# Softmax attention beside linear attention on one core: the DMA-made exponent copy against a third copy on VectorE

## The chip, the core and the metric

The kernel runs on one core of a Trainium2 chip. TensorE (PE) multiplies matrices into PSUM, ScalarE (ACT) and VectorE (DVE) do element-wise work and read PSUM, GpSimd (POOL) does element-wise work in SBUF, and SyncE (SP) issues most transfers; GpSimd can issue transfers too. PSUM has eight banks of 128 x 512 fp32. Each engine runs its own instruction list in order, and semaphores tie the lists together. The metric is the device time of one execution in microseconds, lower being better.

## The reference

Two attention layers on different inputs, with 2048 rows, width 512 and 32 heads of 16; their outputs stand side by side.

```
A:  q,k,v = split(x @ wqkv);  p = softmax(q k^T / 4);  out_A = (p v) @ wo
B:  q,k,v = split(x @ wqkv);  pq = q w_phi;  pk = k w_phi            (per head)
    phi(t) = [softmax(t), softmax(-t)]                               (32 features)
    kv = phi(pk)^T v;  z = sum_s phi(pk);  out_B = (phi(pq) kv / (phi(pq) z + 1e-6)) @ wo
```

A has 32 x 2048 x 2048 = 134 million exponentials and is by far the larger part. B is linear in the sequence.

## The kernel before

**Units and key tiles.** Part A is cut into 32 units: 4 query chunks of 512 rows times 8 groups of 4 heads. A unit has 16 key tiles of 128 keys, so there are 512 key tiles. For each, PE makes four score pieces (one head each, 128 keys x 512 queries, `kq`, L771), an engine takes their exponentials, and PE multiplies these with the values (`pv_task`, L778); a 17th column of ones in the value tile `VP` makes the softmax's row sums. Four heads sit side by side in the array, in row strips for the scores and in column strips for the products.

**Two ways to the exponential.** ACT takes it with its own function, two or three pieces an instruction (`act_exp`, L1003), into the tile `pT`. DVE [...]writes a scaled and rounded score as a 16-bit integer into `rg` (L1061) and the bits are then read as fp16: that is a power of two with a straight line between powers. To mend the straight line, the kernel takes four such numbers, whose integers are shifted by 0, 256, 512 and 768 (`sh`), each multiplied with a value tile scaled by a fitting weight (`VP` and the three `VJ`), and lets PE add up the four products. So a key tile on DVE (`dve_kt`) needs four conversions, three shifted copies, and four products on PE instead of one. Only the key tiles in `DK`, five of each unit, may go this way; 136 of the 512 did.

**How the copies are made.** Copies 2 and 3 are one DVE instruction each on the whole tile of 128 x 2048 integers (L1079). Copy 1 is made by the DMA engines: SP fills a slot of `rg` with the constant 256 from `sh_d` in DRAM (`pf`, L1071), and GpSimd then issues a transfer from the first tile to that slot which adds as it writes (`ac`, L1073). `rg` has eight slots: `NB = 3` for first tiles, `NJ = 2` for DVE's copies, `ND = 3` for the DMA's. A first tile's slot becomes free when its product and all of its copies are done.

**End of a unit.** DVE copies the products' bank to `X` (L831). SP moves the row sums to `sums` (L839), DVE takes reciprocals (`rin`, L847), SP writes these to DRAM (`scr`, L850) and reads them back broadcast over the partitions (`Yd`, L853), and GpSimd multiplies (L869), into `OT` for even groups or `Oo` for odd ones, whose rows SP then moves into `OT` (L876). `X` and `Yd` have two slots each. When a chunk's eight groups are done, PE applies `wo` (L1124), DVE evacuates to `OA` (L1139) and SP stores.

**Part B** runs in the gaps of part A: projections with folded weights, exponentials on ACT (L1226, L1293), sums, divisions and products on DVE and GpSimd (L1231 to L1340), its output projection on PE (L1352).

**What sets the order.** A small planner in the program (`_Sched`) fixes every engine's instruction list ahead of time. Each kind of work is a stream of tasks with an assumed duration. The planner always places the task that can start first, shifted by a weight of its stream; the weights come from `_W`, and `_AT` changes them after so many key tiles of progress. The planner also decides which key tiles DVE gets (`src_d`, `cut`, `lead`, `dg`), and it adds products with a tile of zeros where PE would be idle too much (`filler`, L805). DVE's copies and GpSimd's instructions are kept apart in the plan (`port`). It assumes 0.59 us for a DVE copy, and 5.0 us for a DMA copy after 1.1 us on GpSimd.

Of the kernel before, what the change touches and what calls it, by code (L numbers as in the profile page):

```python
# [161 lines left out]
class _Sched:  # L162
# [147 lines left out]
    def _place(self, t, start):  # L310
# [41 lines left out]
        if t.then is not None:  # L352
# [4 lines left out]
          b=-0.067, op=-0.004, dx=-0.205, dxe=-0.193, dev=-0.248, dop=-0.359, dn=-0.214, da=-0.165, dad=0.113,  # L357
# [2 lines left out]
          aqf=-0.089, aot=-0.317, age=0.03, early=0.0, guard=0.346, cut=5, lead=6, b0=0.286, b1=0.54, b2=0.99,  # L360
          p0=8, p1=30, p2=6.012, el=2, va=8, ka=4, dm=0.4, force=0.41, fill=0.575, dg=9.0)
_AT = (
    (24, dict(qa=-0.125, qd_o=0.203, da=-0.187, df=-0.11, aot=-0.35)),
    (48, dict(qd_o=0.356, pa_n=2, dev=-0.104, kv=0.078)),
    (72, dict(tp=-0.294, qd_r=0.065, qd_o=0.321, pa_w=0.123, dx=-0.302, dred=-0.087, dv=-0.001, dmn=0.142,
         akf=0.041, aot=-0.47, lead=7)),
    (96, dict(qa=-0.159, da=-0.247, kf=-0.02, y=-0.153, t=0.012, df=0.019, dred=-0.109, dd=-0.017, dob=0.004,
         aqf=0.01, guard=0.283, force=0.419, dg=3.0)),
    (120, dict(tp=-0.226, qa=-0.04, qd_r=0.073, qd_o=0.235, pa_n=3, pa_w=0.053, dx=-0.205, dev=-0.248, da=-0.165,
         kf=-0.03, kv=0.004, y=-0.203, t=0.061, df=-0.163, dred=-0.076, dv=-0.053, dd=0.003, dob=-0.078, dmn=0.041,  # L370
         akf=-0.019, aqf=-0.089, aot=-0.317, guard=0.346, lead=6, force=0.41, dg=9.0)),
    (144, dict(dy=0.009, aot=-0.297, guard=0.274, lead=5)),
    (168, dict(qd_r=-0.022, pa_n=2, dn=-0.167, dv=-0.125, dd=-0.063, akf=-0.032, aqf=-0.171, fill=0.586, dg=3.0)),
    (192, dict(qd_r=0.097, y=-0.085)),
    (216, dict(qa=-0.039, qd_r=0.115, pj=-0.014, pa_n=3, dxe=-0.133, dev=-0.306, dn=-0.214, dad=0.045, y=-0.203,
         dv=-0.014, dy=-0.02, dd=0.003, dmn=-0.032, akf=-0.019, aqf=-0.089, aot=-0.317, guard=0.346, el=3,
         fill=0.597, dg=1.5)),
    (240, dict(qd_r=0.14, pa_n=4, pd_w=0.153, da=-0.114, df=-0.266, dob=-0.175, dmn=0.08, aqf=-0.079, guard=0.248)),
    (264, dict(dx=-0.377, dad=0.025, akf=-0.119)),
    (288, dict(tp=-0.301, pa_n=5, pd_w=0.016, dad=-0.034, kf=0.01, v=0.055, qf=-0.094, y=0.004, df=-0.336,  # L380
         dmn=0.121)),
    (312, dict(op=0.063, dad=-0.024)),
    (336, dict(y=-0.045, df=-0.392)),
    (360, dict(op=-0.021, kf=0.025, o=0.205, dd=0.064)),
    (384, dict(kf=-0.024, guard=0.269)),
    (408, dict(dxe=-0.193, t=0.163, cut=4, lead=4)),
    (432, dict(qd_o=0.185, pj=0.163, b=-0.08, op=-0.003, dop=-0.46, v=0.03, kv=-0.04, y=0.001, t=0.272, o=0.12,
         df=-0.395, dd=-0.028, aot=-0.427, lead=5, dg=0.8)),
    (456, dict(tp=-0.219, qd_r=0.146, pa_n=6, b=-0.094, op=-0.009, dn=-0.244, kv=-0.137, t=0.295, dob=-0.155,
         dmn=0.138, aqf=-0.026, guard=0.311, cut=5, lead=4, force=0.427)),  # L390
    (480, dict(tp=-0.226, qd_r=0.115, qd_o=0.235, pj=-0.051, pa_n=4, pd_w=0.104, b=-0.067, op=-0.004, dx=-0.255,
         dev=-0.139, dop=-0.359, dn=-0.214, da=-0.165, dad=0.113, kf=-0.03, v=0.039, kv=0.004, qf=-0.012, y=-0.203,
         t=0.061, o=0.243, df=-0.163, dv=-0.053, dd=0.003, dob=-0.125, dmn=0.041, akf=-0.019, aqf=-0.089,
         aot=-0.383, guard=0.483, lead=6, el=2, force=0.415, fill=0.575, dg=9.0)),
    (504, dict(qd_o=0.219, pa_n=2, dx=-0.277, dev=-0.248, df=-0.133, dob=-0.029, aot=-0.317, guard=0.346,
         force=0.41, fill=0.62)),
)
# [8 lines left out]
def _main_path(nc, es, P, dsem, flag, A_x, A_wqkv, A_wo, B_x, B_wqkv, B_w_phi, B_wo, out):  # L406
# [1 line left out]
    S, H, NG, NKT, NQC = 2048, 32, 8, 16, 4  # L408
    NU = NG * NQC
    VW = H * 17  # L410
    NPT = 13
    NB, NJ, ND = 3, 2, 3
    NR = NB + NJ + ND
    DK = (3, 6, 9, 12, 15)
    units = [(g, c) for c in range(NQC) for g in range(NG)]
    MM = _Sched.MM
# [3 lines left out]
    def sb(name, shape, dt):  # L420
        return es.enter_context(nc.sbuf_tensor(name, shape, dt))
# [44 lines left out]
    QT = sb("QT", [128, NQC, 4, 512], BF)  # L466
    KT = sb("KT", [128, NG, S], BF)
    OT = sb("OT", [128, 2, 4, 512], BF)
    Oo = sb("Oo", [128, 1, 512], BF)
    VP = sb("VP", [128, NKT, VW], BF)  # L470
    VJ = sb("VJ", [128, _NPH - 1, len(DK), VW], BF)
    WOp = sb("WOp", [128, 4, 512], BF)
# [4 lines left out]
    Yd = sb("Yd", [128, 2, 512], F32)  # L477
    sums = sb("sums", [128, 512], F32)
    rin = sb("rin", [128, 2, 16], F32)
    OA = sb("OA", [128, 1, 512], BF)  # L480
    zer = sb("zer", [128, 32], BF)
    scr = nc.dram_tensor("scr", [NU, 4, 512], F32)
    sh_d = nc.dram_tensor("sh_d", [1, 2048], U16)

    A_bank = [_Slot(0), _Slot(3)]
    G = [_Slot(5), _Slot(6), _Slot(7), _Slot(2)]
    beside = {0: (G[3], 0), 3: (G[3], 2)}
    pt_sl = [_Slot(i) for i in range(NPT)]
    rg_sl = [_Slot(i) for i in range(NR)]
    ri_sl, rj_sl, rd_sl = rg_sl[:NB], rg_sl[NB:NB + NJ], rg_sl[NB + NJ:]  # L490
    x_sl = [_Slot(i) for i in range(2)]
    y_sl = [_Slot(i) for i in range(2)]
    oo_sl = [_Slot(i) for i in range(1)]
    r_sl = [_Slot(i) for i in range(2)]
    oa_sl = [_Slot(i) for i in range(1)]

    def left_in(slots, lo, wt):
        def f(_):
# [29 lines left out]
    po_n = SC.stream("pool", 0.0)  # L528
    po_k = SC.stream("pool", 0.0)
    po_v = SC.stream("pool", 0.02)  # L530
    po_a = SC.stream("pool", -0.3)
    sp_q = SC.stream("sp", 0.0)
    sp_pf = SC.stream("sp", -0.05)
    ac_q = SC.stream("act", -1.0)
    sp_b = SC.stream("sp", 0.01)
    sp_bo = SC.stream("sp", 0.01)
# [15 lines left out]
    def dma(key, fn, n=1):  # L552
        def emit(t, toks):
            tok = None
            for i in range(n):
                tok = P.dma("sp", key(t) if callable(key) else key, lambda e, i=i: fn(e, t, i), toks)
            return tok
        return emit

    def sw(key, fn):  # L560

        def emit(t, toks):
            return P.dma("pool", key(t), lambda e: fn(e, t), toks)
        return emit

    d_pf = [dsem("pf%d" % i) for i in range(ND)]
    d_ac = [dsem("ac%d" % i) for i in range(ND)]

    def put(s, t):
        s["q"].append(t)  # L570
        return t
# [33 lines left out]
    for s in y_sl:  # L605
        s.toks = [t_yd1]
    t_zer = P.op("pool", lambda e: e.memset(zer[:], 0.0))
    t_sh = P.op("pool", lambda e: e.memset(rg[0:1, NR - 1, :], float(sh[1])))
    l_sh = load("shc", lambda e, i: e.dma_start(sh_d[:], rg[0:1, NR - 1, :]), 0.5, pre=[t_sh])
    rd_sl[-1].toks = [t_sh]  # L610
    t_vp1 = P.op("pool", lambda e: e.memset(VP[:].rearrange("p k (h j) -> p k h j", j=17)[:, :, :, 16], 1.0))
    SC.free["pool"] = 5.0
    SC.free["pe"] = 1.0
# [151 lines left out]
    def v0(h):  # L765
        return 17 * h - 16 * (h % 2)
# [263 lines left out]
    def dve_kt(u, kt):  # L1030
# [40 lines left out]
        pf = put(sp_pf, _Task("sp", 0.5, dma(lambda t: d_pf[t.res["j"].idx - NB - NJ], lambda e, t, i: e.dma_start(  # L1071
            rg[:, t.res["j"].idx, :], sh_d[:].broadcast_to([128, 2048]))), [l_sh], lat=3.3, need=[("j", rd_sl, 1, 1)]))
        ac = put(po_a, _Task("pool", 1.1, sw(lambda t: d_ac[pf.res["j"].idx - NB - NJ], lambda e, t: e.dma_start(  # L1073
            rg[:, pf.res["j"].idx, :], rg[:, q0.res["i"].idx, :], accum_op=ALU.add)), [pf] + firsts, lat=5.0,
            rel=[lambda: [q0.res["i"]]]))
        put(pe_pd, pv_task(u, [ac, vj_ready[(kt, 1)]], lambda h: VJ[:, 0, k, v0(h):v0(h) + 32],
                           lambda r: tile(pf.res["j"], r), [lambda: [pf.res["j"]]]))
        for j in range(2, _NPH):
            ad = put(dv_ad, _Task("dve", 0.59, one("dve", lambda e, t, j=j: e.tensor_scalar(  # L1079
                rg[:, t.res["j"].idx, :], rg[:, q0.res["i"].idx, :], float(sh[j]), 32767.0, ALU.add, ALU.min)),  # L1080
                firsts, lat=DL, need=[("j", rj_sl, 1, 1)], rel=[lambda: [q0.res["i"]]], port=True))
# [65 lines left out]
    woB = sb("woB", [128, 4, 512], BF)  # L1147
    Wf = sb("Wf", [128, 2, 4, 512], BF)
    e_k = sb("e_k", [128, 2, 1024], BF)
    eT = sb("eT", [128, 2, 2, 512], BF)  # L1150
    KVacc = sb("KVacc", [128, 272], F32)
    KVbd = sb("KVbd", [128, 8, 144], BF)
    rmin = sb("rmin", [128, 64], F32)
# [8 lines left out]
    o_b = [wfl[:, 4352 + 512 * k:4864 + 512 * k] for k in range(2)]  # L1162
    oT_b = [e_k[:, k, 0:512].rearrange("p (t s) -> p t s", s=128) for k in range(2)]
    ob_b = [e_k[:, k, 512:1024] for k in range(2)]
    eT_b = [eT[:, k] for k in range(2)] + [Wf[:, 1, 2 * k:2 * k + 2, :] for k in range(2)]
    et_sl = [_Slot(k) for k in range(4)]
    d_ob = [dsem("ob0"), dsem("ob1")]

    pe_kf, pe_v, pe_kv, pe_qf, pe_y, pe_t, pe_o = (SC.stream("pe", x) for x in "kf v kv qf y t o".split())
# [1217 lines left out]
```

## Time and profile before

| What | Value |
|---|---|
| Three runs | 944.51, 947.09, 932.78 us; median 944.51 |
| Profiled execution | 944.51 us, of which the span of instructions is 942.8 us |
| Busy | PE 788.4, ACT 749.9, DVE 690.0, POOL 312.7 us |
| Mean clock granted to TensorE | 0.869 of full |
| Bytes moved by DMA | 166.05 MB, mean 176 GB/s |
| Of these read from or written to HBM | 83.12 and 4.45 MB |
| Prefill of copy 1, SP | 136 times, 5.6 us to landing |
| Accumulation of copy 1, GpSimd | 136 times, 6.0 us to landing |
| DVE conversions, copies | 544 of 681 ns, 272 of 736 ns (means) |

A row of the groups names line, engine, operation, output and inputs, shape and count; after the bar stand the busy time in us, the mean of one in ns, and the engine's idle time just before these instructions with what ended it. A row of the waits names who waited for what, the total in us, how often, and the longest. PE is shown as matmuls (PE) and weight loads (PEld). Records of two instructions that follow each other can overlap a little, so the busy time of a group can be less than count times mean.

### The profile page before, as it was taken

Reading aid. Unit: us, or ns where it says so; the run is one execution under the profiler, and the core shown is the slowest. Engines: PE = TensorE matmul, PEld = TensorE weight load, DVE = VectorE, ACT = ScalarE, POOL = GpSimd, SP = SyncE. Lnnn points to the kernel's source line nnn. Section 1 sums busy time; section 2 is a strip of 40 time slices with the busy share of each in tenths; the row PEclk is TensorE's granted clock in tenths of the full one; section 3 lists DMA queues with packets and bytes.
Section 4 is the critical chain, followed back from the end, with each engine's and each line's share of the span. In section 5 each row is a group of like instructions: output and inputs, shape, how many; then the busy total and the mean of one; then the engine's idle time right before and its main releaser. Section 6 shows DMA issues by size and latency. Waiting matters only on the chain.

```text
span 942.8 us, 17573 instructions
## 1 busy us (share of the span) xinstructions
PE 788.4 (84%) x7172; PEld 220.1 (23%) x7251; DVE 690.0 (73%) x1214; ACT 749.9 (80%) x821; POOL 312.7 (33%) x399
## 2 busy tenths in 40 slices
PE   9898787888688869888898977987987987897986
PEld 3221122222122212222222222222321221232222
DVE  3787787778186668787778878787875885688674
ACT  6797797788588959778888878887976885798884
POOL 4333232321123334433333233133452312343430
PEclk9997899889798979778969989799987896799699
DMA  6777787879776856877767887877664885869563
GB/s 147 200 179 165 185 212 175 188 172 212 208 185 173 201 129 167 195 170 182 192 158 182 216 189 189 192 173 187 160 157 111 198 215 138 199 158 217 131 153 85
DMA packets 83045, 166.05 MB, mean 176 GB/s; under 512 B 35533, under 2 KB 44173, under 8 KB 82958
## 3 DMA queue, kind: packets, MB, share of 16 engines
q0 software_dynamic: 19584, 71.31, 41.2%
q1 hardware_dynamic: 63374, 93.55, 32.8%
q8 instruction: 58, 0.95, 0.4%
q14 instruction: 29, 0.24, 0.1%
HBM read 83.12 MB, written 4.45 MB: 93 GB/s over the span
## 4 chain that ended last, share of the span: by engine, by line
DMA 37%; PE 28%; DVE 16%; issue 6%; ACT 6%; POOL 3%; SPq 3%; POOLq 0%; DVEq 0%
DMA rg<-rg 17%; PE PS L778 12%; PE PS L771 10%; DVE rg L1061 7%; DMA sums<-X 7%; ACT pT L1003 6%; DMA Yd<-scr 5%; DVE rg L1079 4%; DMA scr<-rin 4%; SPq L596 2%; DMA out_dram<-OA 2%; DMA rg<-sh_d 2%; POOL OT L869 1%; DVE X L831 1%; PE PS L1249 1%
## 5 line engine op out<-in xcount | busy, mean ns | idle before, releaser
L1003 ACT ACTIVATE pT<-PS 128x1024 bf16<-128x1024 f32 (+1 forms) x740 | 715.0, 1064 | 174.0 <-PE PS L771 171.1
L1061 DVE TENSOR_SCALAR rg<-PS 128x512 uint16<-128x512 f32 x544 | 355.6, 681 | 104.9 <-PE PS L771 102.3
L771 PE MATMUL PS<-QT,KT 32*128 32x512 bf16 x2048 | 337.5, 427 | 43.8 <-DMA rg<-rg 11.6
L1073 POOL DMA_DIRECT2D rg<-rg x136 | 125.3, 922 | 371.2 <-DVE rg L1061 180.7
L778 PE MATMUL PS<-rg,VJ 128*32 128x512 f16 x1632 | 168.4, 439 | 61.6 <-DMA rg<-rg 57.4
L1079 DVE TENSOR_SCALAR rg<-rg 128x2048 uint16<-128x2048 uint16 x272 | 194.2, 736 | 16.5 <-PE PS L778 15.4
L778 PE MATMUL PS<-pT,VP 128*32 128x512 bf16 x1504 | 163.8, 432 | 5.1 <-ACT pT L1003 2.2
L771 PEld LDWEIGHTS PS<-QT,KT 32*128 32x128 bf16 x2048 | 78.6, 92 | 351.1 <-ACT pT L1003 171.7
L778 PEld LDWEIGHTS PS<-rg,VJ 128*32 128x32 bf16 x1632 | 39.8, 99 | 130.3 <-DMA rg<-rg 70.2
L778 PEld LDWEIGHTS PS<-pT,VP 128*32 128x32 bf16 x1504 | 39.3, 97 | 89.3 <-issue 64.5
L778 PE MATMUL PS<-rg,VP 128*32 128x512 f16 x544 | 59.8, 430 | 0.3 <-DVE rg L1061 0.3
L869 POOL TENSOR_TENSOR OT<-X,Yd 128x256 bf16<-128x256 f32 x30 | 22.2, 756 | 77.5 <-DMA Yd<-scr 68.0
L869 POOL TENSOR_TENSOR Oo<-X,Yd 128x256 bf16<-128x256 f32 x30 | 25.7, 868 | 56.1 <-DMA Yd<-scr 56.1
L831 DVE COPY X<-PS 128x512 f32<-128x512 f32 (+1 forms) x33 | 22.0, 670 | 26.5 <-PE PS L778 18.6
L1240 POOL TENSOR_TENSOR w<-e_k,stat 128x512 bf16<-128x512 bf16 x32 | 35.6, 1175 | 14.4 <-DVE rg L1079 7.0
L661 PE MATMUL PS<-xT,w 128*128 128x512 bf16 x102 | 33.6, 406 | 5.3 <-issue 2.6
L847 DVE RECIPROCAL rin<-sums 128x16 f32<-128x16 f32 x31 | 7.7, 248 | 35.9 <-DMA sums<-X 35.7
L1231 POOL TENSOR_TENSOR w<-e_k 128x256 f32<-128x256 bf16 x32 | 22.8, 770 | 14.9 <-PE PS L1260 8.1
L1330 POOL TENSOR_TENSOR w<-w 128x272 f32<-128x272 f32 x32 | 26.5, 905 | 2.8 <-DVE rmin L1321 2.6
L1340 POOL TENSOR_TENSOR w<-w,den 128x256 bf16<-128x256 f32 x32 | 21.8, 726 | 16.6 <-PE PS L1346 7.6
L1316 DVE TENSOR_TENSOR w<-PS,stat 128x408 f32<-128x408 f32 (+1 forms) x48 | 25.1, 522 | 0.8
L805 PE MATMUL PS<-ones_t,zer 128*32 128x512 bf16 x232 | 23.6, 416 | 0.0
(113 smaller groups left out, 477.7 us busy)
## 6 DMA issues: line engine op xcount, KB each, us to landing
rg<-sh_d SPq DMA_DIRECT2D x136, 512.0 KB, 5.6
rg<-rg POOLq DMA_DIRECT2D x136, 512.0 KB, 6.0
Yd<-scr SPq DMA_DIRECT2D x31, 256.0 KB
out_dram<-e_k SPq DMA_DIRECT2D x16, 128.0 KB, 4.1
out_dram<-OA SPq DMA_DIRECT2D x12, 128.0 KB, 3.8
OT<-Oo SPq DMA_DIRECT2D x60, 16.0 KB, 2.6
w<-in_A_wqkv_dram SPq DMA_DIRECT2D x2, 384.0 KB, 4.4
OT<-in_A_x_dram SPq DMA_DIRECT2D x1, 512.0 KB, 4.3
```

The lines of the kernel that those rows point to most:

```text
L661: return e.matmul(bank_of(t), w[:, ct, c0:c0 + 128], xT[:, ct, c * 512:(c + 1) * 512], start=(ct == 0), stop=(ct == 3))
L771: return e.matmul(out_ap, KT[32 * r:32 * r + n, g, kt * 128:(kt + 1) * 128], QT[32 * r:32 * r + n, c, g // 2, :], start=True, stop=True, t ...
L778: return e.matmul(PS[32 * r:32 * r + 32, pvb[u].idx, :], lhs(8 * (g // 2) + 2 * r + g % 2), rhs(r), start=t.res["first"], stop=t.res["last ...
L831: xvs.append(_Task("dve", 0.34 if last else 0.61, one("dve", lambda e, t, k=k: e.tensor_copy(X[:, xvs[0].res["x"].idx, n * k:n * k + n], P ...
L869: ms.append(put(po_n, _Task("pool", 0.7, one("pool", lambda e, t, cs=cs: e.tensor_tensor(OT[:, c % 2, g // 2, cs] if even else Oo[:, ms[0] ...
L1003: return e.activation(pT[:, p:p + n, :].rearrange("p a n -> p (a n)"), PS[:, b:b + n, :].rearrange("p a n -> p (a n)"), ACT.Exp, scale=0.25)
L1061: return e.tensor_scalar(rg[:, q0.res["i"].idx, 512 * r:512 * r + 512], PS[:, qk.res["D"].idx, :], ya, yb, ALU.mult, ALU.add)
L1073: ac = put(po_a, _Task("pool", 1.1, sw(lambda t: d_ac[pf.res["j"].idx - NB - NJ], lambda e, t: e.dma_start(rg[:, pf.res["j"].idx, :], rg[: ...
L1079: ad = put(dv_ad, _Task("dve", 0.59, one("dve", lambda e, t, j=j: e.tensor_scalar(rg[:, t.res["j"].idx, :], rg[:, q0.res["i"].idx, :], flo ...
L1240: ph.append(put(po_phi, _Task("pool", 1.03, one("pool", lambda e, t, a=a: e.tensor_tensor(pk[hs[0].res["k"].idx][:, 512 * a:512 * a + 512] ...
L1316: muls.append(put(dv_y, _Task("dve", 0.485, one("dve", lambda e, t, yv=yv, lo=lo, n=n: e.tensor_tensor(ysv[r0.res["y"].idx][:, 136 * lo:13 ...
L1330: ad = [put(po_y, _Task("pool", 0.73, one("pool", lambda e, t, k=k: e.tensor_tensor(y3(0)[:, 2 * k:2 * k + 2], y3(0)[:, 2 * k:2 * k + 2], ...
```

## The change

The change makes copy 1 on DVE, as copies 2 and 3, and drops what the DMA path needed: `pf`, `ac`, the constant in DRAM, three slots and their semaphores. The room in SBUF goes to other buffers: `rg` has six slots (two for first tiles, four for copies), `pT` 15 slots instead of 13, `Oo` and `OA` two instead of one, and part B's `eT` six instead of four. The table `_AT` is another one, with steps of 16 key tiles instead of 24. The change was named after the first loads, GpSimd's sums in B and the last unit's chain; the code of these three is the same in both files.

```diff
 _AT = (
-    (24, dict(qa=-0.125, qd_o=0.203, da=-0.187, df=-0.11, aot=-0.35)),
-    (48, dict(qd_o=0.356, pa_n=2, dev=-0.104, kv=0.078)),
...
+    (16, dict(dev=-0.308, dv=-0.102)),
+    (32, dict(qa=-0.068, qd_o=0.188, pa_w=0.044, pd_w=0.099, op=-0.026, dop=-0.272, dn=-0.165, da=-0.004,
+         kf=-0.059, v=-0.043, df=-0.078, dred=-0.059, aot=-0.298, cut=4, lead=7, el=3)),
...
-    NPT = 13
-    NB, NJ, ND = 3, 2, 3
-    NR = NB + NJ + ND
+    NPT = 15
+    NB, NJ = 2, 4
+    NR = NB + NJ
...
-    Oo = sb("Oo", [128, 1, 512], BF)
+    Oo = sb("Oo", [128, 2, 512], BF)
...
-    OA = sb("OA", [128, 1, 512], BF)
+    OA = sb("OA", [128, 2, 512], BF)
...
-    sh_d = nc.dram_tensor("sh_d", [1, 2048], U16)
...
-    ri_sl, rj_sl, rd_sl = rg_sl[:NB], rg_sl[NB:NB + NJ], rg_sl[NB + NJ:]
+    ri_sl, rj_sl = rg_sl[:NB], rg_sl[NB:]
...
-    t_sh = P.op("pool", lambda e: e.memset(rg[0:1, NR - 1, :], float(sh[1])))
-    l_sh = load("shc", lambda e, i: e.dma_start(sh_d[:], rg[0:1, NR - 1, :]), 0.5, pre=[t_sh])
-    rd_sl[-1].toks = [t_sh]
...
-        pf = put(sp_pf, _Task("sp", 0.5, dma(lambda t: d_pf[t.res["j"].idx - NB - NJ], lambda e, t, i: e.dma_start(
-            rg[:, t.res["j"].idx, :], sh_d[:].broadcast_to([128, 2048]))), [l_sh], lat=3.3, need=[("j", rd_sl, 1, 1)]))
-        ac = put(po_a, _Task("pool", 1.1, sw(lambda t: d_ac[pf.res["j"].idx - NB - NJ], lambda e, t: e.dma_start(
-            rg[:, pf.res["j"].idx, :], rg[:, q0.res["i"].idx, :], accum_op=ALU.add)), [pf] + firsts, lat=5.0,
-            rel=[lambda: [q0.res["i"]]]))
-        put(pe_pd, pv_task(u, [ac, vj_ready[(kt, 1)]], lambda h: VJ[:, 0, k, v0(h):v0(h) + 32],
-                           lambda r: tile(pf.res["j"], r), [lambda: [pf.res["j"]]]))
-        for j in range(2, _NPH):
+        for j in range(1, _NPH):
             ad = put(dv_ad, _Task("dve", 0.59, one("dve", lambda e, t, j=j: e.tensor_scalar(
                 rg[:, t.res["j"].idx, :], rg[:, q0.res["i"].idx, :], float(sh[j]), 32767.0, ALU.add, ALU.min)),
                 firsts, lat=DL, need=[("j", rj_sl, 1, 1)], rel=[lambda: [q0.res["i"]]], port=True))
...
-    eT = sb("eT", [128, 2, 2, 512], BF)
+    eT = sb("eT", [128, 4, 2, 512], BF)
...
-    eT_b = [eT[:, k] for k in range(2)] + [Wf[:, 1, 2 * k:2 * k + 2, :] for k in range(2)]
-    et_sl = [_Slot(k) for k in range(4)]
+    eT_b = [eT[:, k] for k in range(4)] + [Wf[:, 1, 2 * k:2 * k + 2, :] for k in range(2)]
+    et_sl = [_Slot(k) for k in range(6)]
```

More of the change, by code (lines that the diff above doesn't have):

```diff
@@ L362 @@
 _AT = (
-    (24, dict(qa=-0.125, qd_o=0.203, da=-0.187, df=-0.11, aot=-0.35)),
-    (48, dict(qd_o=0.356, pa_n=2, dev=-0.104, kv=0.078)),
[L365 to L394, printed above, removed]
@@ L395 @@
-    (504, dict(qd_o=0.219, pa_n=2, dx=-0.277, dev=-0.248, df=-0.133, dob=-0.029, aot=-0.317, guard=0.346,
-         force=0.41, fill=0.62)),
+    (16, dict(dev=-0.308, dv=-0.102)),
+    (32, dict(qa=-0.068, qd_o=0.188, pa_w=0.044, pd_w=0.099, op=-0.026, dop=-0.272, dn=-0.165, da=-0.004,
+         kf=-0.059, v=-0.043, df=-0.078, dred=-0.059, aot=-0.298, cut=4, lead=7, el=3)),
+    (48, dict(qd_o=0.109, pj=0.016, pa_n=2, pd_n=1, da=-0.077, dad=0.04, av=-0.032, dv=-0.246, guard=0.228,
+         force=0.38, fill=0.556)),
@@ new lines @@
+    (64, dict(pa_n=3, op=-0.037, dad=0.036, kf=-0.243, y=-0.225, cut=3, fill=0.573)),
+    (80, dict(tp=-0.15, qa=-0.181, dx=-0.007, dv=-0.271, akf=-0.129, aot=-0.311, cut=4)),
+    (96, dict(qd_o=0.141, pj=0.02, pd_w=0.04, b=-0.131, dx=-0.195, dn=-0.057, av=-0.048, v=-0.065, qf=0.031,
+         dd=-0.021, fill=0.623)),
+    (112, dict(pd_n=2, b=-0.217, dxe=-0.202, dev=-0.401, dn=0.184, da=0.018, av=-0.154, kf=-0.257, v=0.028,
+         y=-0.134, dv=-0.252, dd=-0.046, dob=-0.065, cut=3)),
+    (128, dict(qd_o=0.134, pa_n=2, dx=-0.124, dxe=-0.159, v=0.004)),
@@ new lines @@
+    (144, dict(pa_w=0.018, dn=0.164, kf=-0.414, qf=0.186, cut=2)),
+    (160, dict(op=0.003, dmn=0.06)),
+    (176, dict(qa=-0.164, pa_w=-0.006, b=-0.343, dop=-0.158, av=-0.143, guard=0.037)),
+    (192, dict(pa_n=3, pa_w=0.008, pd_n=0, dn=0.248, av=-0.182, qf=0.305, dred=-0.031, dy=0.026, dmn=0.073)),
+    (208, dict(pj=-0.009, op=-0.102, dx=-0.133, dop=-0.198, da=-0.038, o=0.245, dmn=0.098, akf=0.006, el=4)),
+    (224, dict(da=-0.031, kf=-0.434, aot=-0.37)),
+    (240, dict(op=-0.093, dxe=-0.227, dop=-0.171, y=-0.161, t=0.169, dred=-0.09, dkv=-0.144, dob=0.072, akf=-0.083,
+         aot=-0.391, cut=3, lead=8, force=0.42)),
@@ new lines @@
+    (256, dict(pj=-0.033, pa_w=0.073, dxe=-0.188, dev=-0.503, dmn=0.116, guard=0.09)),
+    (272, dict(dn=0.115, dob=0.081)),
+    (288, dict(dx=-0.188, v=-0.027, dy=0.063, dd=0.023)),
+    (304, dict(av=-0.153, y=-0.14, dd=0.033)),
+    (320, dict(b=-0.239, da=-0.05, v=-0.037, kv=-0.099, qf=0.191, dred=-0.107)),
+    (336, dict(dn=0.212)),
+    (352, dict(pa_n=4, da=-0.076, y=-0.124, fill=0.606)),
+    (368, dict(qd_o=0.035, pd_n=1, op=-0.129, t=0.088, df=-0.063)),
+    (384, dict(pj=-0.119, dop=-0.114, o=0.226, force=0.416)),
@@ new lines @@
+    (400, dict(dop=-0.045, y=-0.08, dred=-0.12, lead=9)),
+    (416, dict(tp=-0.189, kf=-0.453, kv=-0.201, qf=0.177, dred=-0.046)),
+    (432, dict(pa_n=5, t=0.077, dg=0.8)),
+    (448, dict(qd_r=0.148, pj=-0.118, pd_w=0.015, dop=0.007, av=-0.124, qf=0.176, dv=-0.348, dmn=0.003,
+         akf=-0.153)),
+    (464, dict(pj=-0.021, dn=0.31, cut=4)),
+    (480, dict(tp=-0.226, qa=-0.039, qd_r=0.108, qd_o=0.235, pj=-0.051, pa_n=3, pa_w=0.046, pd_w=0.17, b=-0.067,
+         op=-0.004, dx=-0.205, dxe=-0.193, dev=-0.248, dop=-0.359, dn=-0.238, da=-0.27, dad=0.113, av=-0.051,
+         kf=-0.03, v=0.039, kv=0.004, qf=-0.012, y=-0.203, t=0.117, o=0.193, df=-0.139, dred=-0.076, dv=-0.053,
+         dkv=-0.118, dy=-0.111, dd=0.003, dob=-0.078, dmn=0.041, akf=-0.019, aot=-0.317, guard=0.346, cut=5,
+         lead=6, el=1, force=0.41, fill=0.562, dg=9.0)),
@@ L397 @@
+    (496, dict(dxe=-0.105, da=-0.285, dad=0.109, t=0.068, dy=-0.041, aqf=-0.177)),
 )
@@ L489, in _main_path @@
     rg_sl = [_Slot(i) for i in range(NR)]
-    ri_sl, rj_sl, rd_sl = rg_sl[:NB], rg_sl[NB:NB + NJ], rg_sl[NB + NJ:]
+    ri_sl, rj_sl = rg_sl[:NB], rg_sl[NB:]
     x_sl = [_Slot(i) for i in range(2)]
     y_sl = [_Slot(i) for i in range(2)]
-    oo_sl = [_Slot(i) for i in range(1)]
+    oo_sl = [_Slot(i) for i in range(2)]
     r_sl = [_Slot(i) for i in range(2)]
-    oa_sl = [_Slot(i) for i in range(1)]
+    oa_sl = [_Slot(i) for i in range(2)]
     def left_in(slots, lo, wt):
@@ L530, in _main_path @@
     po_v = SC.stream("pool", 0.02)
-    po_a = SC.stream("pool", -0.3)
     sp_q = SC.stream("sp", 0.0)
-    sp_pf = SC.stream("sp", -0.05)
     ac_q = SC.stream("act", -1.0)
@@ L558, in dma @@
         return emit
[L560 to L567, printed above, removed]
     def put(s, t):
```

## The prediction

> **What bounds the kernel now.** I read the page first (busy shares), then the groups by shape, then who waited for whom, then the PE clock stretch by stretch, and last the timeline at the places where everything stops.
>
> ```profile
> span 942.8 us, 17573 instructions
> ...
> PE 788.4 (84%) x7172; PEld 220.1 (23%) x7251; DVE 690.0 (73%) x1214; ACT 749.9 (80%) x821; POOL 312.7 (33%) x399
> ...
> q0 software_dynamic: 19584, 71.31, 41.2%
> q1 hardware_dynamic: 63374, 93.55, 32.8%
> ```
>
> No engine is full: ACT idles 193 us, DVE 253 us. The DMA engines are busy 74% of the time, although the kernel's inputs and outputs are small; q0 holds nothing but the accumulating copies.
>
> ```profile
> L1003 ACT ACTIVATE pT<-PS 128x1024 bf16<-128x1024 f32 x716 | 684.2, 1050 | 160.4 <-PE PS L771 157.7 <-PE PS L778 0.4
> L1061 DVE TENSOR_SCALAR rg<-PS 128x512 uint16<-128x512 f32 x544 | 355.6, 681 | 104.9 <-PE PS L771 102.3
> ...
> L1079 DVE TENSOR_SCALAR rg<-rg 128x2048 uint16<-128x2048 uint16 x272 | 194.2, 736 | 16.5 <-PE PS L778 15.4 <-PE PS L1260 0.8
> ...
> L1073 POOL DMA_DIRECT2D rg<-rg x136 | 125.3, 922 | 371.2 <-DVE rg L1061 180.7 <-DVE rg L1079 75.6 <-DMA rg<-sh_d 40.4
> ```
>
> ACT and DVE both wait for PE's scores (L771). So the question is what holds PE, which runs its list in order:
>
> ```profile
> ACT pT L1003 <- PE PS L771: 171.1, 150, 6.2
> ...
> PE PS L778 <- DMA rg<-rg: 57.4, 32, 3.4
> ...
> PE PS L771 <- DMA rg<-rg: 11.6, 4, 3.4
> ...
> DVE rin L847 <- DMA sums<-X: 35.7, 13, 6.2
> ...
> SPq L1071 <- PE PS L778: 214.8, 76, 10.5
> ```
>
> PE stands 69 us on the copy that the DMA engines make. DVE stands 36 us on the small transfer of the row sums; SP, which issues it, is held 215 us at the head of its queue by the copy's prefill (L1071). What these stops cost is more than their length, as the clock shows. I laid one set of windows on the 33 stretches at clock 0.50 and one on what lies between them; these are the two sum lines (window, then PE, PEld, DVE, ACT, POOL busy):
>
> ```profile
> sum 246.25, PE 210.75 PEld 44.40 DVE 139.60 ACT 137.11 POOL 71.97; mean PE 6.39 PEld 1.35 DVE 4.23 ACT 4.15 POOL 2.18
> ```
> ```profile
> sum 696.52, PE 577.62 PEld 175.69 DVE 550.36 ACT 612.83 POOL 240.69; mean PE 17.50 PEld 5.32 DVE 16.68 ACT 18.57 POOL 7.29
> ```
>
> In 246 us PE has half its clock, and there ACT works 56% and DVE 57% of the time; in the other 697 us ACT works 88% and DVE 79%. Setting the start of each half-clock stretch beside PE's stop just before it: 20 of them, 167 us, follow a stop on the DMA copy; 8, 61 us, follow a stop behind another late transfer (row sums, reciprocals, the odd head's rows, an output row); 5, 18 us, anything else. One of the second kind, in the timeline:
>
> ```profile
> 329.94 0.25 DVE L847 RECIPROCAL rin<-sums 128x16 f32<-128x16 f32 x1 [5.52 <-DMA sums<-X]
> ...
> 331.89 0.58 PE L771 MATMUL PS<-QT,KT 32*128 32x512 bf16 x1 [4.36 <-DVE rmin L1246]
> ```
>
> DVE waits 5.5 us for 8 KB, PE then waits for DVE, and from 331.3 its clock is half for 6.8 us.
>
> **What the Trainium skill says.** "TensorE: Matmul & The Clock Gate" (Part 1): the clock is either full or half, decided in windows of about 3.4 us by PE's activity. The trace agrees: only 1.00 and 0.50 occur, and the stretches are multiples of 3.4 us. "DMA: Bandwidth & Descriptors" (Issuing engines are not separate DMA queues): SP's and GpSimd's transfers share the same 16 engines and interleave. The trace agrees: row sums of 8 KB land in 2 to 10 us. "VectorE: DVE Perf Modes" (the perf-mode tier table): a tensor_scalar on 2,048 16-bit elements in SBUF takes 693 ns; here 683 median. "SBUF — State Buffer" (Who interferes with whom): in that mode VectorE takes ports that GpSimd needs, and one blocks the other. That fits the mean of 736 over the median of 683.
>
> **The change part by part**, against the profiled run (span 942.8, time 944.51, which is also the median of the three).
>
> *Removed: copy j=1 by DMA.* 136 prefills from SP, 136 accumulations from GpSimd (125.3 us busy), 71.3 MB on q0 and 136 x 0.512 = 69.6 MB on q1, 141 of 166 MB. Three waits go: PE's 69 us; SP's at L1071 (215 us and 72 us more behind L771), so that sums, reciprocals and broadcasts leave when ready; GpSimd's at L1073, which held its multiplications. If all DMA-caused half-clock stretches went, 18 us would be left; if only those of the copy, 79. I take 70, since the row sums still make three transfers one after the other, now on nearly empty engines.
>
> *Added: copy j=1 on DVE.* 194.2/272 = 0.714 us each, port conflicts included; 136 x 0.714 = 97 us. This is on no idle engine: DVE would come to 787 of 943. Bounds: 0.602 (the usual start-to-start of two such copies) gives 82 us, 0.736 gives 100.
>
> *How the planner shares it out.* The program orders the work with a greedy planner, which can hand a key tile to ACT instead of DVE. A key tile costs ACT 715.0 x 4/1504 (both shapes) = 1.90 us, and 34.9 us other work; on DVE 355.6/136 = 2.615 us plus copies, and 140 us other work. With three copies, 34.9 + 1.90(512-N) = 140 + (2.615 + 2.142)N gives N = 130 and 760 us on both. If N stays at 136: ACT 750, DVE 787. If it drops to 120: 780 and 711. I take 760 on both.
>
> *Buffers.* First tiles 3 to 2: before, such a tile stays in use through the DMA's 6.0 us; now 3 x 0.6 us of copies follow the four conversions, so two should do; cost 0, at worst a conversion waiting for a matmul, some 0.4 us x 130 = 52 us. Copy tiles 2 on DVE to 4: DVE's 15.4 us behind L778 lessen; gain 0 to 15. pT 13 to 15: ACT waits 0.4 us for L778, so 0. Output rows and odd-head rows 1 to 2 each: up to 3.2 us (output rows) and a part of PE's single 6.0 us stop for the odd rows. eT 4 to 6: no row shows a wait on it, 0. I put 0 to 10 of this in the range.
>
> *The tables of weights* (`_AT`) reorder every engine's list. No row prices that. An estimate: ACT's share differs between full-clock stretches of like work (0.96 from 355 to 383 us, 0.93 from 557 to 587), so the order is worth half of that, 1.5% or 14 us, either way; 0 taken.
>
> *New waits.* PE's product with copy 1 now waits for DVE; behind it on PE are the next scores, and behind those ACT. On DVE, the third copy stands ahead of conversions that free a score bank, and ahead of the X copy that closes a unit.
>
> *The rest of the change's name* (first loads, GpSimd's k sums, last unit's chain) is the same code in both files: 0. Near the start, a 1.8 us memset on GpSimd and one SP load go, beside other work.
>
> *Sum.* Time = C + (760 - 0.56 C)/u, with C the half-clock time and u the share that both engines reach at full clock. ACT reached 0.88 with DVE at 0.79; now both are needed, so I take u = 0.865: with C = 70, 70 + 721/0.865 = 903; with the 1.7 us around the span, 905. u = 0.90 and C = 18 give 853; u = 0.84 and C = 79 give 933.
>
> **Rivals.**
> *(A) Forecast:* stops and cold stretches go; 905.
> *(B) Only the copy's own stops go*, row sums and broadcasts stay late by their own latency: C = 110, u = 0.86: 110 + 698/0.86 + 2 = 924. For: three dependent transfers. Against: their landing times swing with the load.
> *(C) No change:* PE's waits on DMA turn into equal waits on DVE, C stays 246: 246 + 622/0.88 + 2 = 955 (at u = 0.89, 947). For: DVE is behind 25 us of PE's stops already, in part its own lateness; against: most of those came from its wait for the sums.
> *(D) Slower:* DVE becomes the bound. N stays 136, DVE has 787 us and, with every third copy ahead of a conversion in its list, reaches over the whole span only the 0.795 that ACT, the busiest of the two, reaches now: 787/0.795 = 990. It decides from the point where DVE's share stays under 787/963 = 0.82. For: DVE's share at full clock was 0.79 with two copies. Against: in the stretch 822.8 to 870.6 ACT reached 0.92 and DVE 0.88 together.
>
> **How the numbers follow.** A 0.42, B 0.13, C 0.19, D 0.26. Within 2% (926 to 963) is what a measurement of this kernel can hardly tell from none. Faster: A and B, 0.55; same: C, 0.19; slower: D, 0.26. Range 868 to 975: below lies a twentieth (the best corner of A), above the worse half of D. A's and B's own range is 868 to 930.
>
> **What would show it.** Right: the mean clock rises from 0.869 to 0.94 or more; no wait on rg<-rg; sums and Yd waits on DVE and GpSimd fall under 15 us each; L1079-like copies near 390 at a mean under 760 ns; DVE and ACT both near 0.84 of the span. Wrong: clock as before, with PE's stops now named after DVE's copies (C), or DVE over 780 us busy with ACT idling over 220 us (D).

## The result and the profile after

The kernel after takes 765.1 us (median of four runs, 763.0 to 767.4); the kernel before took 944.2 (median of four, 932.8 to 947.1). The ratio is 0.814, with a 95% interval of 0.806 to 0.822. The same kernel has slower executions now and then, so a run more than 1.5% above the fastest of its kernel is left out of the ratios and of the times below. The prediction said 905 with a range of 868 to 975. The direction was right; the gain is 179 us instead of 39, and the time lies far below the range.

The page of the kernel after, the lines that answer to those shown of before (busy time with its share of the span, clock, DMA queue):

```profile
span 761.4 us, 17199 instructions
...
PE 712.4 (94%) x7117; PEld 215.7 (28%) x7203; DVE 722.8 (95%) x1308; ACT 742.2 (97%) x841; POOL 179.9 (24%) x262
...
PEclk9999999999999999999999999999999999999999
...
q1 hardware_dynamic: 43788, 22.24, 10.8%
```

ACT and DVE are nearly full, and the clock is whole in every slice. q0 is gone, and of 166 MB 23 are left. Leaving out the start and the end, one window says it best (PE, PEld, DVE, ACT, POOL busy, then clock, DMA share, GB/s):

```profile
25.00:738.00 713.00, 670.41 (x6843) 200.32 (x6923) 695.55 (x1250) 708.99 (x802) 171.93 (x241) 1.00 0.09 25
```

ACT works 709 of 713 us and DVE 696. The groups by shape:

```profile
L995 ACT ACTIVATE pT<-PS 128x1024 bf16<-128x1024 f32 x752 | 701.4, 1131 | 2.4 <-PE PS L763 2.0
L1053 DVE TENSOR_SCALAR rg<-PS 128x512 uint16<-128x512 f32 x520 | 334.8, 679 | 8.1 <-PE PS L763 6.7
...
L1064 DVE TENSOR_SCALAR rg<-rg 128x2048 uint16<-128x2048 uint16 x390 | 257.6, 699 | 0.3
```

DVE makes 390 copies instead of 272, for 130 key tiles instead of 136. The 160 us for which ACT stood before its exponentials of two pieces have become 2.4. The waits have turned round, since now PE's weight loads wait for ACT, in short pieces:

```profile
PEld PS L763 <- ACT pT L995: 269.2, 659, 0.8
POOL OT L861 <- DMA Yd<-scr: 110.7, 10, 36.8
...
POOL Oo L861 <- DMA Yd<-scr: 49.3, 6, 21.3
...
PEld PS L770 <- DVE rg L1064: 19.0, 74, 0.5
...
DVE rg L1053 <- PE PS L763: 6.7, 21, 1.1
```

Waits for ACT of at most 0.8 us cost nothing, since ACT is the bound. GpSimd waits longer than before for `Yd`, because it comes to its multiplication early and has nothing else to do. DVE no longer waits for the row sums at all.

### The profile page after: what moved, and what is told of

Its sections match the earlier page's. It is cut to its first block, busy times and chain, and to the rows that moved or that the text cites. A ratio compares the mean times of both kernels' runs of the same rounds, so it can differ in the third digit from the quotient of the medians.

```text
span 761.4 us, 17199 instructions
## 1 busy us (share of the span) xinstructions
PE 712.4 (94%) x7117; PEld 215.7 (28%) x7203; DVE 722.8 (95%) x1308; ACT 742.2 (97%) x841; POOL 179.9 (24%) x262
## 4 chain that ended last, share of the span: by engine, by line
ACT 77%; PE 13%; DVE 6%; DMA 2%; issue 1%; POOL 1%; POOLq 0%
ACT pT L995 73%; PE PS L763 4%; PE PS L770 3%; DVE rg L1053 2%; PE PS L653 2%; ACT e_k L1211 2%; ACT eT L1278 2%; DVE rg L1064 2%; PE PS L650 1%; DMA Yd<-scr 1%; PE PS L607 1%; PE PS L916 0%; PE PS L1337 0%; ACT Wf L1278 0%; DMA scr<-rin 0%
## 5 line engine op out<-in xcount | busy, mean ns | idle before, releaser
L995 ACT ACTIVATE pT<-PS 128x1024 bf16<-128x1024 f32 x760 | 711.4, 1134 | 2.4 <-PE PS L763 2.0
L1053 DVE TENSOR_SCALAR rg<-PS 128x512 uint16<-128x512 f32 x520 | 334.8, 679 | 8.1 <-PE PS L763 6.7
L763 PE MATMUL PS<-QT,KT 32*128 32x512 bf16 x2048 | 315.3, 384 | 24.8 <-ACT pT L995 18.9
L1064 DVE TENSOR_SCALAR rg<-rg 128x2048 uint16<-128x2048 uint16 x390 | 257.6, 699 | 0.3
L770 PE MATMUL PS<-pT,VP 128*32 128x512 bf16 x1528 | 150.9, 387 | 1.7 <-ACT pT L995 0.3
L770 PE MATMUL PS<-rg,VJ 128*32 128x512 f16 x1560 | 144.0, 385 | 0.6 <-DVE rg L1064 0.2
L770 PE MATMUL PS<-rg,VP 128*32 128x512 f16 x520 | 51.2, 384 | 0.5 <-DVE rg L1053 0.2
L861 POOL TENSOR_TENSOR Oo<-X,Yd 128x256 bf16<-128x256 f32 x30 | 21.3, 729 | 75.6 <-DMA Yd<-scr 49.3
L689 POOL TENSOR_SCALAR KT<-KT,hmask 128x512 bf16<-128x512 bf16 x12 | 8.4, 696 | 59.4 <-DVE KT L663 34.3
L1211 ACT ACTIVATE e_k<-PS 128x512 bf16<-128x512 f32 x32 | 19.8, 752 | 0.2 <-PE PS L1208 0.2
```

What stands on the lines that cost most here:

```text
L763: return e.matmul(out_ap, KT[32 * r:32 * r + n, g, kt * 128:(kt + 1) * 128], QT[32 * r:32 * r + n, c, g // 2, :], start=True, stop=True, t ...
L770: return e.matmul(PS[32 * r:32 * r + 32, pvb[u].idx, :], lhs(8 * (g // 2) + 2 * r + g % 2), rhs(r), start=t.res["first"], stop=t.res["last ...
L861: ms.append(put(po_n, _Task("pool", 0.7, one("pool", lambda e, t, cs=cs: e.tensor_tensor(OT[:, c % 2, g // 2, cs] if even else Oo[:, ms[0] ...
L995: return e.activation(pT[:, p:p + n, :].rearrange("p a n -> p (a n)"), PS[:, b:b + n, :].rearrange("p a n -> p (a n)"), ACT.Exp, scale=0.25)
L1053: return e.tensor_scalar(rg[:, q0.res["i"].idx, 512 * r:512 * r + 512], PS[:, qk.res["D"].idx, :], ya, yb, ALU.mult, ALU.add)
L1211: exps = [put(ac_kf, _Task("act", 0.49, one("act", lambda e, t, a=a: e.activation(e_k[:, f.res["e"].idx, 512 * a:512 * a + 512], bank_of(f ...
```

## The experiments

Two accounts stood against each other. The **load theory**: the copy's traffic makes transfers late, each late one stops the in-order lists, and the half clock lengthens the stop. The **plan theory**: the new table and the larger buffers carry a large part. A third, the **latency theory**, came out of the plan's own figures: the plan assumed 5.0 us for a copy that takes 6.0, and only PE's wait on that copy mattered.

### Only the copy moved

```diff
-    NB, NJ, ND = 3, 2, 3
+    NB, NJ = 3, 5
...
-        pf = put(sp_pf, ...
-        ac = put(po_a, ...
-        for j in range(2, _NPH):
+        for j in range(1, _NPH):
```

> The kernel before with one thing changed: copy 1 is made on DVE, with three slots for first tiles and five for copies; table, pT, Oo, OA and eT as before. Load theory (the traffic of the copy makes transfers late, each late one stops PE, and the half clock multiplies the stop): clock over 0.97, 765 to 800 us, so at least four fifths of the 179 us gained. Plan theory (the new table and the larger buffers carry a large part): 830 us or more, with waits left on buffers.

Measured: 781.9 us (ratio 0.832, 0.823 to 0.841), clock 0.986. With the table and the other buffers of before, this is a gain of 17% where the whole change gains 19%, so nine tenths of it.

### Only the old table

```diff
 _AT = (
-    (16, dict(dev=-0.308, dv=-0.102)),
+    (24, dict(qa=-0.125, qd_o=0.203, da=-0.187, df=-0.11, aot=-0.35)),
...
```

> The kernel after with the table of weights of before, all else as after. Load theory: 765 to 790 us at a clock over 0.97. Plan theory: over 800 us, DVE or ACT idling more than 80 us.

Measured: 780.6 us (ratio 0.830, 0.823 to 0.838), clock 0.998. The table is worth some 15 us, which is little more than the noise of the two ratios. DVE idled 71 us there (775.5 less 704.9), just under the plan theory's mark.

### Only the small buffers

```diff
-    NPT = 15
+    NPT = 13
...
-    Oo = sb("Oo", [128, 2, 512], BF)
+    Oo = sb("Oo", [128, 1, 512], BF)
...
-    OA = sb("OA", [128, 2, 512], BF)
+    OA = sb("OA", [128, 1, 512], BF)
...
-    eT = sb("eT", [128, 4, 2, 512], BF)
+    eT = sb("eT", [128, 2, 2, 512], BF)
```

> The kernel after with the small buffers of before (pT 13, Oo and OA one each, eT four), its own table, and rg as after. Load theory: 765 to 780 us, the clock at 0.97 or more. Plan theory: over 790 us.

Measured: 786.2 us (ratio 0.835, 0.828 to 0.841), clock 0.988. That is above what the load theory gave and below the plan theory's mark: the buffers are worth some 21 us. Table and buffers are therefore small, and the plan theory falls. Their worths do not add up: the run in which only the copy moved lacks both and stands 17 us behind the kernel after, though its `rg` has eight slots instead of six. This kernel is the base for the runs with added traffic, which need its room.

### The traffic without a reader

```diff
-    NB, NJ = 2, 4
+    NB, NJ, ND = 2, 4, 2
...
+        pf = put(sp_pf, _Task("sp", 0.5, dma(lambda t: d_pf[t.res["j"].idx - NB - NJ], lambda e, t, i: e.dma_start(
+            rg[:, t.res["j"].idx, :], sh_d[:].broadcast_to([128, 2048]))), [l_sh], lat=3.3, need=[("j", rd_sl, 1, 1)]))
+        put(po_a, _Task("pool", 1.1, sw(lambda t: d_ac[pf.res["j"].idx - NB - NJ], lambda e, t: e.dma_start(
+            rg[:, pf.res["j"].idx, :], WOp[:].rearrange("p t n -> p (t n)").bitcast(U16), accum_op=ALU.add)),
+            [pf, l_wo] + firsts, lat=5.0, rel=[lambda: [pf.res["j"]]]))
         for j in range(1, _NPH):
```

> The kernel with small buffers of the run beside it, copies all on DVE, plus the same prefill and accumulating transfer for every key tile on DVE, into two slots that nobody reads (the transfer adds a stored weight tile; results unchanged). PE waits for none of it. Load theory: row sums and broadcasts land in 4 to 10 us again, PE stops behind them, clock 0.85 to 0.95, 810 to 900 us. Latency theory (only PE's own wait on a copy that lands later than the plan assumed mattered, the load on other transfers did not): within 2% of the run with small buffers and no such traffic, clock over 0.97.

Measured: 923.3 us, clock 0.885. That is slower than even the load theory's 900. Nothing waits for these copies on PE, DVE or ACT, and yet they take back 137 of the 179 us (923.3 less 786.2). The latency theory falls: PE's own wait on the copy, with 69 us the longest of PE's DMA stops before, was not the heart of it. GpSimd and SP do stand at these transfers; whether that matters is the next section's question. The timeline shows how DVE and PE stop behind a small transfer while the large ones run:

```profile
243.53 0.54 SPq L846 DMA_DIRECT2D sums<-X  x1
...
255.23 0.25 DVE L854 RECIPROCAL rin<-sums 128x16 f32<-128x16 f32 x1 [12.48 <-DMA sums<-X]
255.40 1.83 DVE L1084 TENSOR_SCALAR rg<-rg 128x2048 uint16<-128x2048 uint16 x3
...
256.09 1.21 PE L785 MATMUL PS<-rg,VJ 128*32 128x512 f16 x8 [11.63 <-DVE rg L1084]
```

SP issues 8 KB of row sums at 243.5. DVE, whose list has the reciprocal next, gets them 11.7 us later, after a wait of 12.5; PE waits 11.6 for the copies behind it. In the waits of the whole run:

```profile
DVE rin L854 <- DMA sums<-X: 48.9, 9, 12.5
```

In the small-buffer kernel without the traffic, and in the kernel after, DVE never waits for `sums`.

### Bytes alone, and who stands

The rest asks what in that traffic does it. The first three runs change one property each; all stand on the small-buffer kernel (786.2 us).

Bytes alone:

```diff
+    NT = 16
...
+        for _ in range(2):
+            pf = _Task("sp", 0.5, dma(lambda t: d_jk[t.res["j"].idx], lambda e, t, i: e.dma_start(
+                junk[t.res["j"].idx], WOp[:].rearrange("p t n -> p (t n)"))), [l_wo], lat=5.0, need=[("j", jk_sl, 1, 1)])
```

> The kernel after with small buffers, plus two plain transfers of 512 KB from a stored weight tile to unused DRAM for every key tile on DVE, all from SP. They wait for no engine, and a slot is used again only 16 transfers later, so neither SP nor GpSimd stands still for them; GpSimd issues none. If the bytes themselves make the small transfers late: 850 to 930 us, clock under 0.95, row sums landing in 4 us or more. If it is the queues (SP and GpSimd standing at a transfer that waits, with other transfers and GpSimd's work behind it): under 815 us at a clock over 0.96.

Measured: 831.1 us, clock 0.965: 45 us more than without the bytes. It meets neither mark: it is short of the 850 that bytes as the only cause would have given, and above the 815 of the queues.

The issues and waits of the traffic without a reader, with 1/32 of the bytes:

```diff
-            rg[:, t.res["j"].idx, :], sh_d[:].broadcast_to([128, 2048]))), [l_sh], ...
+            rg[:, t.res["j"].idx, 0:64], sh_d[:, 0:64].broadcast_to([128, 64]))), [l_sh], ...
...
-            rg[:, pf.res["j"].idx, :], WOp[:].rearrange("p t n -> p (t n)").bitcast(U16), accum_op=ALU.add)),
+            rg[:, pf.res["j"].idx, 0:64], WOp[:, 0, 0:64].bitcast(U16), accum_op=ALU.add)),
```

> The kernel with the copy's traffic and no reader (same prefill and accumulation for every key tile, same waits, same issue on SP and GpSimd), but only 64 of the 2048 columns, 1/32 of the bytes. If the bytes matter: within 3% of the kernel after with small buffers (786), clock over 0.96. If the queues and their waits matter by themselves: over 840 us.

Measured: 791.0 us, clock 0.989. Issue, queue order and waits cost some 5 us at most; without the bytes they are harmless, and with them the same list takes 923.3.

SP made to stand, against the run with bytes alone:

```diff
-    NT = 16
+    NT = 2
```

> As the run with bytes alone (831 us), but the two transfers for every key tile share two slots instead of 16, so SP stands at its queue's head until the last transfer but one has landed. Bytes, GpSimd and PE's waits as there. If SP's standing, with row sums and broadcasts behind it, is what turns slow bytes into stops: 870 to 940 us, SP standing over 200 us at this line. If it is not: 820 to 840 us.

Measured: 804.7 us, clock 0.980. The wait of SP at this line:

```profile
SPq L1070 <- DMA junk<-WOp: 180.3, 108, 6.0
```

SP stands for 180 us, and the kernel is faster than with 16 slots. I had held SP's standing for part of the cause; here it is not one. That it spreads the bytes more evenly would fit, but was not shown.

GpSimd's accumulating transfer in the place of the second plain one:

```diff
-        for _ in range(2):
...
+        put(po_a, _Task("pool", 1.1, sw(lambda t: d_ak[pf.res["j"].idx], lambda e, t: e.dma_start(
+            junk[pf.res["j"].idx], WOp[:].rearrange("p t n -> p (t n)"), accum_op=ALU.add)), [pf] + firsts, lat=5.0,
+            rel=[lambda: [pf.res["j"]]]))
```

> As the run with bytes alone (831 us), but the second of the two transfers is an accumulating one issued by GpSimd, which waits for the first to land and for the four conversions; 16 slots, so SP hardly stands. If GpSimd's standing (its multiplications behind it) or the accumulating transfer's own load on the DMA engines matters: 870 to 940 us, with DVE and PE waiting for GpSimd or row sums landing late. If not: 820 to 845 us.

Measured: 901.6 us, clock 0.896: 115 of the 137 us are back. This could be GpSimd's standing or the accumulation, so two more runs part these.

Accumulating without waits:

```diff
-            ... accum_op=ALU.add)), [pf] + firsts, lat=5.0,
+            ... accum_op=ALU.add)), [l_wo], lat=5.0, need=[("k", ak_sl, 1, 1)]))
```

> As the run in which GpSimd issues accumulating transfers (902 us), but they wait for nothing, neither for the prefill nor for the conversions, and have 16 slots of their own; the bytes and their kind are the same. If the accumulating transfers' load on the DMA engines makes the others late: 870 to 910 us again. If GpSimd's standing was it: 820 to 845 us.

Measured: 883.7 us, clock 0.908: 98 us over the kernel without traffic.

Waits without accumulating:

```diff
-            junk[pf.res["j"].idx], WOp[:].rearrange("p t n -> p (t n)"), accum_op=ALU.add)), [pf] + firsts, lat=5.0,
+            junk[pf.res["j"].idx], WOp[:].rearrange("p t n -> p (t n)"))), [pf] + firsts, lat=5.0,
```

> As the run in which GpSimd issues accumulating transfers (902 us), with all their waits, but the transfers are plain: same bytes, nothing added up. If accumulating is what loads the DMA engines: 820 to 850 us, and q0's share well below the 45.7% seen there. If GpSimd's standing, or software-made transfers of any kind, are it: 880 to 910 us.

Measured: 817.8 us, clock 0.972: 32 us over it. So most of what these transfers cost comes from the accumulation, and not from GpSimd's waits. The DMA queues of the two runs with GpSimd's waits show its load on the engines; first accumulating, then plain (packets, MB, share of 16 engines' span):

```profile
q0 software_dynamic: 17856, 65.02, 45.7%
q1 hardware_dynamic: 61644, 87.26, 28.6%
```
```profile
q1 hardware_dynamic: 61644, 87.26, 31.3%
q0 software_dynamic: 17856, 65.02, 20.4%
```

The same 65.02 MB in the same number of packets take 0.457 x 898.9 us of the engines against 0.204 x 816.1: 411 us against 166, or 2.5 times. These transfers write to unused DRAM, where the kernel before accumulates into `rg` in SBUF, but the load is alike: q0 took 5.4 us of all engines per MB there (0.412 x 942.8 over 71.31) and takes 6.3 accumulating and 2.6 plain here. By these shares the DMA engines are 74% busy in the one run and 52% in the other; before, it was 74%. A share is the time of packets, which can overlap (a window of 14 us of the kernel before has 1.19), so it is a measure of load and not a limit.

### The kernel before with a quarter of the bytes

```diff
...
-            rg[:, t.res["j"].idx, :], sh_d[:].broadcast_to([128, 2048]))), [l_sh], lat=3.3, ...
+            rg[:, t.res["j"].idx, 0:512], sh_d[:, 0:512].broadcast_to([128, 512]))), [l_sh], lat=3.3, ...
...
-            rg[:, pf.res["j"].idx, :], rg[:, q0.res["i"].idx, :], accum_op=ALU.add)), [pf] + firsts, lat=5.0,
+            rg[:, pf.res["j"].idx, 0:512], rg[:, q0.res["i"].idx, 0:512], accum_op=ALU.add)), [pf] + firsts, lat=5.0,
```

> The kernel before with copy 1 made for a quarter of its columns (512 of 2048; the rest of copy 1 is left at a constant, so that part of the sum is left out), with all waits, issues and slots as before. Load theory: the clock over 0.95 and 790 to 850 us, PE's wait on the copy under 25 us. If the fixed length of a transfer and the chain of three waits bind and not the bytes: over 890 us.

Measured: 773.0 us, clock 0.978, better than the load theory had it. The table, small buffers, slots, waits and 136 key tiles on DVE are those of before, and PE's wait on the copy is 1.4 us:

```profile
L779 PE MATMUL PS<-rg,VJ 128*32 128x512 f16 x1632 | 150.3, 393 | 3.3 <-DVE rg L1080 1.9 <-DMA rg<-rg 1.4
```

This is the shortest proof that the bytes are the cause: three quarters of them are worth 165 us (938.2 less 773.0). It takes away the lateness of the copy and that of the other transfers together; only the run without a reader parts the two.

### A plan that knows the late landings

```diff
-            rg[:, t.res["j"].idx, :], sh_d[:].broadcast_to([128, 2048]))), [l_sh], lat=3.3, ...
+            rg[:, t.res["j"].idx, :], sh_d[:].broadcast_to([128, 2048]))), [l_sh], lat=6.5, ...
...
-            ... accum_op=ALU.add)), [pf] + firsts, lat=5.0,
+            ... accum_op=ALU.add)), [pf] + firsts, lat=8.5,
```

and the three transfers at a unit's end to 6.0, 4.0 and 8.0 us.

> The kernel before with later landings assumed in the plan: prefill 6.5 us instead of 3.3, accumulation 8.5 instead of 5.0, row sums 6.0 instead of 2.6, reciprocals 4.0 instead of 2.2, broadcast 8.0 instead of 2.6. Work, bytes and buffers as before. If a plan that knows the late landings can hide them (the fault was the assumption, not the traffic): under 850 us, clock over 0.95. If the landings swing too much or the slots don't reach: 880 to 960 us.

Measured: 856.3 us (ratio 0.912), clock 0.948, between both marks. With no work moved off the DMA engines, a truer assumption wins back 83 of the 179 us. The planner answered it with other lists, in which DVE has 118 key tiles instead of 136, so 147 MB move instead of 166; but the load hardly changed (173 GB/s against 176), and ACT has 20 us more work. The load and the assumption are two halves of one cause: late transfers stop a list that was written for punctual ones. What even this plan doesn't hide are the swings; its copies land in 6.1 us at the median and in up to 10.9.

### The clock by itself

```diff
-        if u is None:
+        if u is None or NOFILL:
             return False
```

> The kernel after without the products with zeros that the planner puts in where PE would be idle. They take part in no result. If the half clock is what turns a short lack of PE work into lost time: half-clock stretches appear (clock 0.70 to 0.93) and the time rises to 800 us or more although no wait was added. If the clock is only a symptom: 755 to 775 us.

Measured: 781.5 us, clock 0.969. Without the products with zeros 48 us of half clock appear, and the time rises by 16 us, less than I gave it. In those 48 us ACT idles 11, where in the kernel after it hardly idles at all. So the half clock seems to cost some time by itself, at most a third of its length here; it is an amplifier and not the cause. This is not the clock quite alone, because the planner orders the rest a little otherwise too (132 key tiles on DVE instead of 130).

### Two tries at a better version

Copy 1 of two key tiles in five on GpSimd:

```diff
...
+            pool = j == 1 and kt in (6, 12)
+            ad = put(po_cp if pool else dv_ad, _Task("pool" if pool else "dve", 2.2 if pool else 0.59,
...
```

> The kernel after with copy 1 of two key tiles in five made by GpSimd, which idles 581 us there. If DVE's 723 us and ACT's 742 us of work are what binds now: DVE gives up about 50 copies of 0.6 us, shared out between both some 15 us, 745 to 760 us. If GpSimd's copy of about 2.2 us blocks DVE's own copies through the shared port: 765 to 800 us, with DVE's copies at a mean over 760 ns.

Measured: 1150.2 us, clock 0.79, far beyond both marks. Two groups and a wait say why:

```profile
L1067 DVE TENSOR_SCALAR rg<-rg 128x2048 uint16<-128x2048 uint16 x331 | 408.2, 1265 | 72.2 <-PE PS L771 69.0 <-PE PS L1248 2.1
L1067 POOL TENSOR_SCALAR rg<-rg 128x2048 uint16<-128x2048 uint16 x56 | 396.4, 7078 | 183.9 <-DVE rg L1067 80.2 <-DVE rg L1054 64.5 <-PE PS L764 15.9
```
```profile
PE PS L771 <- POOL rg L1067: 202.5, 48, 5.1
```

GpSimd's copy takes 7.1 us and not the 2.2 of the plan, so PE stands 203 us at products that the plan held for ready. DVE's own copies rise to a mean of 1265 ns, because 41 of them take 3.1 to 7.0 us. The Trainium skill ("SBUF — State Buffer", Who interferes with whom) says that VectorE, in the fast mode of such copies, and GpSimd exclude each other: whichever comes second waits for the first one's end. The trace agrees: each of the 41 starts during a copy of GpSimd's and ends 0.55 us after that copy does, and no copy of DVE's that starts in one is short. That is far stronger than the 53 ns between mean and median that I had read it from.

Copy 1 of one key tile in five on the DMA engines:

```diff
...
+        by_dma = kt == 9
+        if by_dma:
...
-        for j in range(1, _NPH):
+        for j in range(2 if by_dma else 1, _NPH):
```

> The kernel after with copy 1 made by the DMA engines for one key tile in five (about a fifth of the bytes of before), planned with 7.0 us to landing; pT 13, OA one, eT four and one slot for the DMA's copy to make room. If a light load is harmless and DVE's work binds: DVE gives up some 26 copies of 0.6 us, half of that in time against the 786 us of small buffers, 765 to 785 us. If even a fifth makes transfers late: 790 us or more.

Measured: 825.2 us (ratio 0.879, 0.868 to 0.890), clock 0.969. The DMA engines are 26% busy here, less than in the run with a quarter of the bytes (36%), which takes 773.0, so the load of the traffic alone hardly explains it. DVE got 119 key tiles and idles 152 us on the span of 827.6, and ACT's work is 769 us against 751 in the small-buffer kernel. The single slot for the DMA's copy, or the table, may have made the planner share out the work so. I did not part these; it is only shown that this version doesn't pay. No version beat the kernel after.

## Why the prediction was right and wrong

**Right:** which wait bound the kernel, and by what way. Late transfers stopped PE and DVE, and the half clock followed; both are gone, and putting back the traffic alone brings both back. N = 130 on DVE came out exactly, as did the copies' count of 390, at a mean of 699 ns where I had taken 714. To the digit that is luck: with three copies on DVE the planner chose 124 with the old table, 127 with the small buffers and 132 without the products with zeros. The table's 14 us either way measured 15.

**Wrong:** the sum's terms, and one of them above all. In the formula Time = C + (760 - 0.56 C)/u the profile after has C = 0, ACT 742 and DVE 723 us of work, and u = 742/761 = 0.975. Taken one after the other, C = 70 to 0 is 25 us, 760 to 742 is 21 (a key tile cost ACT 1.86 us and not 1.90), and u = 0.865 to 0.975 is 97. The step that failed is this one: "ACT reached 0.88 with DVE at 0.79; now both are needed, so I take u = 0.865". I read the idle 12% at full clock as what three in-order lists cost each other by nature. They cost 0.6% in the window shown above. Before, ACT idled 84 us at full clock; after, it idles 19 us in the whole span, start and end included. That most of those 84 came from the same late transfers is shown by the run with a quarter of the bytes: same table, same waits, same shares of work, and ACT idles 40 us in all (773.3 less 733.5), against 193. In its 738 us at full clock ACT works 713, a share of 0.965 where the kernel before had 0.88. So the split by the clock put a part of the loss on the undisturbed side.

**The bound of C:** I kept 70 us of half clock, because three transfers still follow each other at a unit's end. On empty engines they come in time: the reciprocals land in 1.4 us at the median where the plan assumes 2.2, DVE never waits for the sums, and no half clock is left.

**Buffers:** I gave them 0 to 10 us; they are worth 21.

**SP's queue:** I held its 215 us at L1071 for a loss. Standing 180 us in the run with two slots, it did no harm.

**Bytes:** the prefills move 71.3 MB as the accumulations do, not 69.6 (a transfer of 512 KB is 0.524 MB), so 142.6 of the 166 MB went. Nothing in the sum hangs on it.

**Rivals.** C and D put DVE's waits or DVE's load in the place of the transfers. PE's weight loads wait for DVE's copies in 74 short pieces of at most 0.5 us, and DVE reaches 0.95, so neither came. B needed the row sums and broadcasts to be late by themselves; they are not. For every rival I judged what lists in order can do from a profile in which they were being disturbed.

**Of "What would show it"** the clock (1.00), the end of the waits on `rg`, DVE's waits for the sums and the copies came true. Two signs failed. The shares are 0.97 and 0.95 and not 0.84, which is the step above seen from the other side. GpSimd's waits for `Yd` rose to 160 us (111 and 49) instead of falling under 15; they were no measure, since that engine now only waits for its next work.

## What to carry to other kernels

A list that is written out ahead of time runs at the speed of its plan only as long as nothing in it comes later than planned, so price a transfer not only by who reads it but by what its load does to every other transfer. When a profile is full of stops, the busy share between the stops is not the ceiling of the undisturbed kernel: work out the time that the busiest engine's work alone would take, and put that into the range. An engine that looks idle (DMA, GpSimd) is not a free place for work if what it does there delays what others wait for.

## What the runs showed of the hardware that I had not expected

- The packets of accumulating transfers took 2.5 times as long as those of plain ones of the same bytes and number (411 against 166 us of all 16 engines for 65 MB).
- 8 KB took 11.7 us from issue to use at one place of the run without a reader, in which the DMA engines are 71% busy over the span.
- On GpSimd a two-operation copy of 128 x 2048 16-bit integers takes 7.08 us, where DVE takes 0.68 (medians), and a copy of DVE's that starts beside it does not end before it.
- ACT and DVE both stayed above 97% for 713 us (709 and 696 us busy), though each waits for PE's scores and PE for both.
